# Talking-heads attention and an MLP in one kernel: relay groups of every 12th or 9th query row, and chunks of 120, 120, 120 and 97 rows

## The chip, the cores and the metric

One core of a Trainium2 chip runs the whole kernel in one launch. The metric is device time in microseconds (us) of that core: the median of three runs.

## The reference

Attention with mixed heads ("talking heads"), then a two-layer MLP with a leaky activation. 4 batches, 12 heads, 448 positions, head size 64; the MLP has 768 inputs and 2048 hidden units. All values are 32-bit floats, except the MLP weights, which the host hands over as 64-bit floats seen as pairs of integers.

```python
scores = scale * np.matmul(q, k.transpose(0, 1, 3, 2))
scores = np.einsum('bhij,hg->bgij', scores, w_pre)
scores = scores - np.max(scores, axis=-1, keepdims=True)
attn = np.exp(scores)
attn = attn / (np.sum(attn, axis=-1, keepdims=True) + 1e-09)
attn = np.einsum('bhij,hg->bgij', attn, w_post)
return np.matmul(attn, v)
...
h = x @ w_in
g = np.maximum(h, 0.0) + alpha * np.minimum(h, 0.0)
return g @ w_out
```

## The kernel before, in words

The kernel has two phases. Phase one (about the first 545 us) is the attention; phase two is the MLP on TensorE, and the change does not touch it.

In phase one the 448 query rows of a batch are cut into four **chunks** (`CHUNKS`, L27). For each chunk the scores of all 12 heads are computed in six products (`qk`, L139), two heads at a time, into PSUM with the query rows on the partitions. Each is copied to the chunk's score tile `st` (`qk_out`, L150): partition = query row of the chunk, and along the partition 12 heads of 448 scores. One partition thus holds 12 x 448 x 4 = 21,504 bytes.

The mixing of heads contracts over heads, so heads have to be on partitions. A **group** is ten query rows; its 10 x 12 = 120 rows of 448 scores are sent by one DMA, the **relay** (`relay`, L159), from ten partitions of `st` to 120 partitions of a small tile `sr`. There are 45 groups per batch, 180 in all, and eight `sr` buffers. Before the change a group's ten rows are ten neighbouring partitions, `st[r:r + 10]`. Relays alternate between the DMA queues of SP and of POOL (GpSimd); the first eight are also dealt to ACT's.

Two groups make a **block** (90 in all). For each block TensorE mixes heads (`mix`, L166, one product per half), VectorE takes the row maxima (`rmax`, L173), ScalarE the exponentials with their sums (`exp`, L178), VectorE the normalisation folded into the second mixing matrix (`norm`, L185), TensorE the second mixing, which also transposes (`post`, L196), and ScalarE copies the result into the chunk's tile `at` (`post_out`, L207), ten columns per group. When a chunk is complete, two products with v (`pv`, L216) follow, each with an output **drain** (`pv_out`, L230): ScalarE copies one PSUM half to `xe`, VectorE adds the other half, and SP stores `xe` to `x2` in DRAM.

Python code writes the order out by hand. `step(m)` issues for block m: loads due in this step, `mix(m + 1)`, stores that the step before left over, the relays up to four blocks ahead, `norm(m - 1)`, `rmax(m + 1)`, `exp(m)`, one q.k or v product with its copy, `post(m - 2)` and further products. The table `jobs`, filled from the chunks' first groups, says which step has which q.k product, v product or load. Each step also runs about 2.6 of the 224 VectorE operations that round the MLP weights (`round_f64`, L41), whose loads (`cr`, POOL's queue) and stores (`wsc`, SP's queue) go on during phase one. q.k and v products share one PSUM buffer (`ps_s`, `bufs=1`), so the next of them waits for the copy or the drain of the last.

The line of the relay, and those of the drain:

```python
dma.dma_start(out=sr_t[n][SR0:SR0 + GP], in_=s_t[ci][r:r + GI])
...
nc.scalar.copy(xe[:, :, :cn], src[:, 0, :, :cn])
nc.vector.tensor_tensor(xe[:, :, :cn], src[:, 1, :, :cn], xe[:, :, :cn], ALU.add)
```

Of the kernel before, what the change touches and what calls it, by code (L numbers as in the profile page):

```python
# [14 lines left out]
ALU = mybir.AluOpType  # L15
# [7 lines left out]
GI = 10  # L23
GP = GI * H
HI = GI // 2
HP = HI * H
CHUNKS = [(0, 110), (110, 110), (220, 110), (330, 118)]  # L27
CW = 118
NCC = DM // 128
NFC = DFF // 128  # L30
NP = H // 2
# [2 lines left out]
SR0 = 4  # L34
# [26 lines left out]
def talking_heads_prelu(ctx: ExitStack, tc: tile.TileContext, q, k, v, w_pre, w_post, mask, w_in, w_out, alpha, out):  # L61
    nc = tc.nc
# [2 lines left out]

    groups, first = [], []
    chunk_list = [(b, c) for b in range(B) for c in range(len(CHUNKS))]
    for ci, (b, c) in enumerate(chunk_list):  # L70
        first.append(len(groups))
        cn = CHUNKS[c][1]
        for r in range(0, cn, GI):
            groups.append((ci, min(r, cn - GI)))
    NG, NC = len(groups), len(chunk_list)
    NB = NG // 2
    first.append(NG)
# [34 lines left out]
    k_t, q_t, v_t, s_t, a_t = {}, {}, {}, {}, {}  # L112
# [8 lines left out]

    def load_q(ci, dmas=None):
        b, c = chunk_list[ci]
        c0, cn = CHUNKS[c]
        q_t[ci] = qp.tile([128, NP, CW], F32, tag="q", name=f"q{ci}")
        for hf in range(2):
            dma = dmas[hf] if dmas else nc.gpsimd
            dma.dma_start(out=q_t[ci][64 * hf:64 * hf + 64, :, :cn],
                          in_=q[b, :, H * c0 + NP * hf * cn:H * c0 + NP * (hf + 1) * cn])
# [7 lines left out]
    u_t = {}  # L137

    def qk(ci, p, ps_pool=None):  # L139
        b, c = chunk_list[ci]  # L140
        cn = CHUNKS[c][1]
        ps = (ps_pool or ps_s).tile([128, 2, 512], F32, tag="m" if ps_pool else "s", name=f"s{ci}_{p}")
# [7 lines left out]
    def qk_out(ci, p, copy=nc.scalar.copy):  # L150
        cn = CHUNKS[chunk_list[ci][1]][1]
        if p == 0:
            s_t[ci] = sp.tile([CW, H, S], F32, tag="s", name=f"st{ci}")
        dst = s_t[ci].rearrange("p (t n) s -> p n t s", t=2)
        copy(dst[:cn, p], u_t.pop(("qk", ci, p))[:cn, :, :S])  # L155

    sr_t, m_t, nm_t, e_t, se_t, r_t = {}, {}, {}, {}, {}, {}

    def relay(n, dma):  # L159
        ci, r = groups[n]  # L160
        sr_t[n] = sr_b[n % NSR]
        dma.dma_start(out=sr_t[n][SR0:SR0 + GP], in_=s_t[ci][r:r + GI])  # L162

    def mix(m):

# [41 lines left out]
    def post_out(m):  # L207
        for g in range(2):
            n = 2 * m + g
            ci, r = groups[n]  # L210
            if n == first[ci]:
                a_t[ci] = ap_.tile([128, NS, H, CW], F32, tag="a", name=f"at{ci}")
            dst = a_t[ci].rearrange("p s h i -> p (s h) i")[:, :, r:r + GI]
            nc.scalar.copy(dst, pa[:, g, :NS * GP].rearrange("p (s i) -> p s i", i=GI))  # L214

    def pv(ci, hx, ps_pool=None):  # L216
        b, c = chunk_list[ci]
        cn = CHUNKS[c][1]
        ps = (ps_pool or ps_s).tile([128, 2, 512], F32, tag="m" if ps_pool else "s", name=f"x{ci}_{hx}")
        for cl in range(3):  # L220
            for s in range(NS):
                for t in range(2):
                    h = 2 * (3 * hx + cl) + t
                    for r in range(2 if 2 * s + 1 < NJ else 1):
                        pr = slice(64 * r, 64 * r + 64)
                        nc.tensor.matmul(ps[64 * t:64 * t + 64, r, cl * CW:cl * CW + cn], v_t[b][pr, s, h * D:(h + 1) * D],  # L226
                                         a_t[ci][pr, s, h, :cn], start=(s == 0), stop=(2 * s + 2 + r >= NJ))
        u_t["pv", ci, hx] = ps

    def pv_out(ci, hx):  # L230
        b, c = chunk_list[ci]
        c0, cn = CHUNKS[c]
        xe = xep.tile([128, 3, CW], F32, tag="xe", name=f"xe{ci}_{hx}")
        src = u_t.pop(("pv", ci, hx))[:, :, :3 * CW].rearrange("p r (c i) -> p r c i", c=3)
        nc.scalar.copy(xe[:, :, :cn], src[:, 0, :, :cn])
        nc.vector.tensor_tensor(xe[:, :, :cn], src[:, 1, :, :cn], xe[:, :, :cn], ALU.add)  # L236
        later.append(lambda: nc.sync.dma_start(
            out=x2[3 * hx:3 * hx + 3, :, b * S + c0:b * S + c0 + cn].rearrange("c p i -> p c i"), in_=xe[:, :, :cn]))

# [32 lines left out]
    for ci, (b, c) in enumerate(chunk_list):  # L272
        if ci:
            m0, m1 = first[ci - 1] // 2 - RAHEAD, first[ci] // 2 - RAHEAD - 2
            for p in range(NP):
                at(max(m0 + p * (m1 - m0) // (NP - 1), p // 2), "qk", ci, p)
        if ci >= 2:
            at(max(first[ci - 2] // 2 - 1, 0), "load", load_q, ci)
        if c == 0:
            if b:  # L280
                at(first[ci] // 2 - 15, "load", load_k, b)
            at(first[ci] // 2 + 3 if b else 1, "load", load_v, b)
        lb = (first[ci + 1] - 1) // 2
        at(lb + LAG + 1, "pv", ci, 0)
        at(lb + LAG + (3 if ci + 1 < NC else 1), "pv", ci, 1)
    conv_steps = NFC * 2 * 7

    with tc.manual_schedule():
        p0 = ExitStack()
        start = p0.enter_context(tc.tile_pool(name="start", bufs=1))  # L290
        hw = (nc.sync, nc.scalar)
        load_q(0, hw)
        load_k(0, ((0, 1), (1, 3), (3, 6)), hw)

# [18 lines left out]
        for i, w in enumerate((w_pre, w_post)):  # L313
            for p in ((SR0, 64), (0, 64))[i]:
                nc.gpsimd.dma_start(out=mask_sb[p:p + HP, i], in_=mask[:HP, :HI, :])
                nc.gpsimd.dma_start(out=wb[p:p + HP, i, :],
                                    in_=w.rearrange("(o h) g -> o h g", o=1).to_broadcast([HI, H, H]))
        load_q(1)
        nc.gpsimd.dma_start(out=alpha_sb, in_=alpha)
        conv = convert()  # L320
        next(conv)
        nc.vector.scalar_tensor_tensor(
            out=wk[:, :HP].rearrange("p (i g) -> p i g", g=H), in0=mask_sb[:, 0], scalar=scale,
# [4 lines left out]
            out=wq.rearrange("p g i -> p i g"), in0=mask_sb[:, 1],  # L328
# [9 lines left out]
        def relays(upto, dmas):  # L338
            nonlocal relayed
            while relayed < min(upto, NG):  # L340
                relay(relayed, dmas[relayed % len(dmas)])
                relayed += 1

        relays(2 * (RAHEAD + 1), (nc.sync, nc.scalar, nc.gpsimd))
        done = 0
        live = lambda m: 0 <= m < NB
        EV = {"qk": (qk, qk_out), "pv": (pv, pv_out)}

        def step(m):
# [23 lines left out]
            if live(m - LAG):  # L373
                post(m - LAG)
                post_out(m - LAG)
# [52 lines left out]
        def l1(u):  # L428
            b, f = divmod(u, NFC)
            w, x = wi_t.pop(u), xs_t[b]  # L430
            ps = P2["h"].tile([128, 512], F32, tag="h", name=f"h{u}")
            i = 0
            for cc in range(NCC):
                for tw, tx in ((0, 0), (0, 1), (1, 0)):
                    nc.tensor.matmul(ps[:, :S], w[:, tw, cc * 128:(cc + 1) * 128], x[:, tx, cc, :],  # L435
                                     start=(i == 0), stop=(i == 3 * NCC - 1))
                    i += 1
            return ps
# [39 lines left out]
        for u in range(NU + 1):  # L478
# [5 lines left out]
            if u < NU:  # L484
                split_w(u, 1)
                ps = l1(u)
# [44 lines left out]
```

## Time and profile before

| what | value |
|---|---|
| median of 3 runs | 1043.7 us (1034.62 to 1052.75) |
| the profiled execution: its own time | 1041.12 us |
| its span, first to last instruction | 1038.9 us |
| TensorE busy over the span | 869.1 us (84%) |
| granted TensorE clock, mean | 0.921 |
| DMA packets | 55209, 123.86 MB |

The profile is of one execution. Busy times are sums of an engine's instructions; PE is TensorE's matmuls, PEld its weight loads, DVE VectorE, ACT ScalarE, POOL GpSimd. A name such as `sr<-st` says what an instruction writes and reads. "idle before" is time in which the engine did nothing just before a group's instructions, and behind it stands what ended that wait; "issue" stands where the profile shows nothing that it waited for. A DMA share is the mean busy share of the core's 16 DMA engines.

### The profile page before, as it was taken

Reading aid. Unit: us, or ns where it says so; the run is one execution under the profiler, and the core shown is the slowest. Engines: PE = TensorE matmul, PEld = TensorE weight load, DVE = VectorE, ACT = ScalarE, POOL = GpSimd, SP = SyncE. Lnnn points to the kernel's source line nnn. Section 1 sums busy time; section 2 is a strip of 40 time slices with the busy share of each in tenths; the row PEclk is TensorE's granted clock in tenths of the full one; section 3 lists DMA queues with packets and bytes.
Section 4 is the critical chain, followed back from the end, with each engine's and each line's share of the span. In section 5 each row is a group of like instructions: output and inputs, shape, how many; then the busy total and the mean of one; then the engine's idle time right before and its main releaser. Section 6 shows DMA issues by size and latency. Waiting matters only on the chain.

```text
span 1038.9 us, 26286 instructions
## 1 busy us (share of the span) xinstructions
PE 869.1 (84%) x11540; PEld 687.8 (66%) x11540; DVE 500.2 (48%) x886; ACT 441.6 (43%) x870; POOL 348.7 (34%) x305
## 2 busy tenths in 40 slices
PE   4656767867868687778666999999999999999998
PEld 2134444544535355455455999999999999999997
DVE  3454666656657376758624224632265224542222
ACT  1453666655657466648342232323233323232322
POOL 3121222222212122211004455554455454545452
PEclk9687898988889798889796999999999999999999
DMA  7698878897899977898618600020001000010001
GB/s 149 154 185 193 173 190 204 220 220 179 167 228 213 200 191 181 186 247 176 145 32 316 271 1 19 1 89 1 1 19 63 27 1 9 9 54 1 1 1 53
DMA packets 55209, 123.86 MB, mean 119 GB/s; under 512 B 21080, under 2 KB 38840, under 8 KB 54712
## 3 DMA queue, kind: packets, MB, share of 16 engines
q0 software_dynamic: 15232, 59.01, 25.7%
q1 hardware_dynamic: 38546, 60.12, 20.7%
q10 hardware_dynamic: 1318, 3.08, 1.2%
q8 instruction: 90, 1.47, 0.6%
q14 instruction: 23, 0.19, 0.1%
HBM read 59.85 MB, written 23.59 MB: 80 GB/s over the span
## 4 chain that ended last, share of the span: by engine, by line
PE 67%; DMA 16%; ACT 7%; issue 5%; DVE 4%; SPq 1%; POOL 0%; ACTq 0%; DVEq 0%; POOLq 0%
PE h L435 23%; PE acc L460 23%; DMA sr<-st 14%; PE s L147 7%; PE x L226 6%; PE m L170 4%; PE pa L204 4%; ACT st L155 3%; ACT at L214 2%; ACT e L182 1%; DMA xr<-x 1%; DMA wb<-in_w_post_dram 1%; DMA cr<-in_w_out_dram 1%; DVE xe L236 1%; DVE nm L175 1%
## 5 line engine op out<-in xcount | busy, mean ns | idle before, releaser
L435 PE MATMUL h<-xs,wi 128*128 128x448 f32 x1152 | 251.4, 371 | 12.6 <-DVE xs L425 11.3
L460 PE MATMUL acc<-g,wo 128*128 128x448 f32 x1152 | 248.2, 368 | 0.0
L435 PEld LDWEIGHTS h<-xs,wi 128*128 128x128 f32 x1152 | 218.4, 190 | 35.4 <-issue 11.5
L460 PEld LDWEIGHTS acc<-g,wo 128*128 128x128 f32 x1152 | 216.2, 188 | 21.8
L413 POOL TENSOR_TENSOR wi<-wr,wi 128x768 fp32r<-128x768 f32 x64 | 118.6, 1853 | 269.8 <-ACT wi L412 269.8
L204 PEld LDWEIGHTS pa<-r,e 64*64 64x64 f32 x5040 | 115.4, 146 | 79.6 <-issue 55.4
L175 DVE TENSOR_REDUCE nm<-m 128x2 f32<-128x896 f32 x90 | 97.9, 1088 | 135.7 <-PE m L170 135.5
L444 DVE TENSOR_SCALAR t<-h,alpha_sb 128x448 f32<-128x448 f32 x64 | 43.8, 684 | 245.7 <-PE h L435 245.7
L204 PE MATMUL pa<-r,e 64*64 64x60 f32 x5040 | 121.9, 234 | 43.6 <-issue 33.8
L170 PE MATMUL m<-sr,wk 64*64 64x448 f32 (+1 forms) x720 | 111.6, 650 | 50.4 <-DMA sr<-st 43.2
L446 ACT CAST g<-t 128x448 fp32r<-128x448 f32 x64 | 36.3, 567 | 275.2 <-DVE t L445 275.2
L162 POOL DMA_DIRECT2D sr<-st x88 | 54.2, 617 | 276.9 <-PE m L170 185.0
L147 PE MATMUL s<-k,q 64*46 64x448 f32 (+2 forms) x768 | 112.7, 640 | 39.5 <-ACT st L155 27.8
L214 ACT COPY at<-pa 128x480 f32<-128x480 f32 x180 | 93.2, 572 | 82.2 <-PE pa L204 82.0
L413 POOL TENSOR_TENSOR wo<-wr,wo 128x768 fp32r<-128x768 f32 x64 | 123.8, 1935 | 7.6 <-ACT wo L412 5.9
L182 ACT ACTIVATE e<-m,nm 128x448 f32<-128x448 f32 x180 | 113.7, 646 | 14.2 <-DVE nm L175 14.2
L226 PEld LDWEIGHTS x<-at,v 64*64 64x64 f32 x2688 | 88.2, 146 | 37.6 <-issue 20.3
L155 ACT COPY st<-s 110x896 f32<-110x896 f32 (+1 forms) x93 | 84.6, 909 | 63.0 <-PE s L147 55.6
L226 PE MATMUL x<-at,v 64*64 64x110 f32 (+1 forms) x2688 | 92.6, 280 | 18.5 <-issue 13.3
L147 PEld LDWEIGHTS s<-k,q 64*64 64x64 f32 (+2 forms) x768 | 27.5, 140 | 92.3 <-ACT st L155 70.9
L170 PEld LDWEIGHTS m<-sr,wk 64*64 64x64 f32 (+1 forms) x720 | 29.3, 151 | 77.5 <-issue 64.7
L412 ACT CAST wo<-wr 128x768 fp32r<-128x768 f32 x64 | 53.8, 841 | 62.3 <-PE acc L460 62.3
(46 smaller groups left out, 564.1 us busy)
## 6 DMA issues: line engine op xcount, KB each, us to landing
sr<-st SPq DMA_DIRECT2D x89, 210.0 KB
sr<-st POOLq DMA_DIRECT2D x88, 210.0 KB, 9.7
cr<-in_w_in_dram POOLq DMA_DIRECT2D x16, 768.0 KB, 11.5
cr<-in_w_out_dram POOLq DMA_DIRECT2D x16, 768.0 KB, 10.1
wsc<-ct SPq DMA_DIRECT2D x32, 384.0 KB
wr<-wsc SPq DMA_DIRECT2D x14, 768.0 KB
xr<-x SPq DMA_DIRECT2D x24, 224.0 KB
out_dram<-o SPq DMA_DIRECT2D x24, 224.0 KB
```

What stands on the lines that cost most here:

```text
L147: nc.tensor.matmul(ps[lo:hi, hf, :S], q_t[ci][r, p, lo:hi], k_t[b][r, p, :], start=True, stop=True)
L155: copy(dst[:cn, p], u_t.pop(("qk", ci, p))[:cn, :, :S])
L162: dma.dma_start(out=sr_t[n][SR0:SR0 + GP], in_=s_t[ci][r:r + GI])
L170: nc.tensor.matmul(ps[hf:hf + 64, u, :S], wk[r, :], g[r, :], start=True, stop=True)
L175: nc.vector.tensor_reduce(out=nm, in_=m_t[m][:, :, :S], axis=AX.X, op=ALU.max, negate=True)
L182: nc.scalar.activation(out=e_t[m][:, u], in_=m_t[m][:, u, :S], func=AF.Exp, bias=nm_t[m][:, u:u + 1], scale=1.0, accum_out=se_t[m][:, u:u ...
L204: nc.tensor.matmul(dst[:, :, HI * u:HI * u + HI], e[h, u, 64 * jb:64 * jb + 64], r[h, u].rearrange("p (h i) -> p h i", h=H), start=True, s ...
L214: nc.scalar.copy(dst, pa[:, g, :NS * GP].rearrange("p (s i) -> p s i", i=GI))
L226: nc.tensor.matmul(ps[64 * t:64 * t + 64, r, cl * CW:cl * CW + cn], v_t[b][pr, s, h * D:(h + 1) * D], a_t[ci][pr, s, h, :cn], start=(s == ...
L413: nc.gpsimd.tensor_tensor(t[:, 1], w, t[:, 0], ALU.subtract)
L435: nc.tensor.matmul(ps[:, :S], w[:, tw, cc * 128:(cc + 1) * 128], x[:, tx, cc, :], start=(i == 0), stop=(i == 3 * NCC - 1))
L460: nc.tensor.matmul(accs[c][:, :S], w[:, tw, c * 128:(c + 1) * 128], g[:, tg], start=(f == 0 and i == 0), stop=(f == NFC - 1 and i == 2))
```

## The change

The chunks become 120, 120, 120 and 97 rows. Group r of one of the first three takes the rows r, r + 12, ... r + 108: ten partitions of `st` that lie 12 apart; twelve groups fill a chunk. The fourth chunk begins at row 351; its nine groups take rows 7 + r, 16 + r, ... 88 + r of the chunk, 9 apart, and its first seven rows are computed in q.k and used by no group. There are still 45 groups per batch, 180 relays and 90 blocks. The columns of `at` now stand group by group, so the drain puts them back in order: it reads PSUM along its columns and writes `xe` in steps of 12 (or 9) elements. Two query rows (358 and 359) are computed and stored by the third and by the fourth chunk.

```diff
--- before.py
+++ after.py
@@ -24,8 +24,9 @@
 GP = GI * H
 HI = GI // 2
 HP = HI * H
-CHUNKS = [(0, 110), (110, 110), (220, 110), (330, 118)]
-CW = 118
+CHUNKS = [(0, 120), (120, 120), (240, 120), (351, 97)]
+ROWS = [(0, 12), (0, 12), (0, 12), (7, 9)]
+CW = 120
 NCC = DM // 128
 NFC = DFF // 128
 NP = H // 2
@@ -65,13 +66,13 @@
     groups, first = [], []
     chunk_list = [(b, c) for b in range(B) for c in range(len(CHUNKS))]
     for ci, (b, c) in enumerate(chunk_list):
         first.append(len(groups))
-        cn = CHUNKS[c][1]
-        for r in range(0, cn, GI):
-            groups.append((ci, min(r, cn - GI)))
+        for r in range(ROWS[c][1]):
+            groups.append((ci, r))
     NG, NC = len(groups), len(chunk_list)
     NB = NG // 2
     first.append(NG)
@@ -121,7 +122,7 @@
     def load_q(ci, dmas=None):
         b, c = chunk_list[ci]
-        c0, cn = CHUNKS[c]
+        c0, cn = sum(n for _, n in CHUNKS[:c]), CHUNKS[c][1]
         q_t[ci] = qp.tile([128, NP, CW], F32, tag="q", name=f"q{ci}")
         for hf in range(2):
             dma = dmas[hf] if dmas else nc.gpsimd
@@ -159,7 +160,9 @@
     def relay(n, dma):
         ci, r = groups[n]
         sr_t[n] = sr_b[n % NSR]
-        dma.dma_start(out=sr_t[n][SR0:SR0 + GP], in_=s_t[ci][r:r + GI])
+        r0, st = ROWS[chunk_list[ci][1]]
+        r0 += r
+        dma.dma_start(out=sr_t[n][SR0:SR0 + GP], in_=s_t[ci][r0:r0 + (GI - 1) * st + 1:st])
     def mix(m):
@@ -210,12 +213,12 @@
             ci, r = groups[n]
             if n == first[ci]:
                 a_t[ci] = ap_.tile([128, NS, H, CW], F32, tag="a", name=f"at{ci}")
-            dst = a_t[ci].rearrange("p s h i -> p (s h) i")[:, :, r:r + GI]
+            dst = a_t[ci].rearrange("p s h i -> p (s h) i")[:, :, r * GI:(r + 1) * GI]
             nc.scalar.copy(dst, pa[:, g, :NS * GP].rearrange("p (s i) -> p s i", i=GI))
     def pv(ci, hx, ps_pool=None):
         b, c = chunk_list[ci]
-        cn = CHUNKS[c][1]
+        cn = ROWS[c][1] * GI
         ps = (ps_pool or ps_s).tile([128, 2, 512], F32, tag="m" if ps_pool else "s", name=f"x{ci}_{hx}")
         for cl in range(3):
             for s in range(NS):
@@ -228,12 +231,16 @@
         u_t["pv", ci, hx] = ps
     def pv_out(ci, hx):
         b, c = chunk_list[ci]
-        c0, cn = CHUNKS[c]
+        r0, st = ROWS[c]
+        c0, cn = CHUNKS[c][0] + r0, st * GI
         xe = xep.tile([128, 3, CW], F32, tag="xe", name=f"xe{ci}_{hx}")
-        src = u_t.pop(("pv", ci, hx))[:, :, :3 * CW].rearrange("p r (c i) -> p r c i", c=3)
-        nc.scalar.copy(xe[:, :, :cn], src[:, 0, :, :cn])
-        nc.vector.tensor_tensor(xe[:, :, :cn], src[:, 1, :, :cn], xe[:, :, :cn], ALU.add)
+        ps = u_t.pop(("pv", ci, hx))[:, :, :3 * CW].rearrange("p r (c i) -> p r c i", c=3)
+        src = [ps[:, r, :, :cn].rearrange("p c (g i) -> p c g i", i=GI) for r in range(2)]
+        dst = xe[:, :, :cn].rearrange("p c (i g) -> p c g i", i=GI)
+        nc.scalar.copy(dst, src[0])
+        nc.vector.tensor_tensor(dst, src[1], dst, ALU.add)
         later.append(lambda: nc.sync.dma_start(
             out=x2[3 * hx:3 * hx + 3, :, b * S + c0:b * S + c0 + cn].rearrange("c p i -> p c i"), in_=xe[:, :, :cn]))
```

Since chunks now begin at other groups, the hand-written order moves. On TensorE, in the last blocks of the first batch's third chunk (`m` is a mixing product, `s_0` to `s_2` the first q.k products of the second batch's first chunk, `pa` the second mixing, `x_1` a v product of the second chunk); before:

```order
L147 MATMUL s_0_1173<-k_627,q_860 64x448 x2
L147 MATMUL s_0_1173<-k_627,q_860 46x448 x2
L147 MATMUL s_1_1180<-k_627,q_860 64x448 x2
L147 MATMUL s_1_1180<-k_627,q_860 46x448 x2
L170 MATMUL m_1193<-sr_116,wk 64x448 x2
L170 MATMUL m_1193<-sr_117,wk 64x448 x2
L147 MATMUL s_2_1213<-k_627,q_860 64x448 x2
L147 MATMUL s_2_1213<-k_627,q_860 46x448 x2
L204 MATMUL pa<-r_1088,e_1042 64x12x5 x28
L170 MATMUL m_1255<-sr_110,wk 64x448 x2
L170 MATMUL m_1255<-sr_111,wk 64x448 x2
L226 MATMUL x_1_1273<-at_677,v_276 64x110 x42
```

and after:

```order
L148 MATMUL s_0_1251<-k_621,q_950 64x448 x2
L148 MATMUL s_0_1251<-k_621,q_950 56x448 x2
L207 MATMUL pa<-r_1144,e_1086 64x12x5 x28
L148 MATMUL s_1_1288<-k_621,q_950 64x448 x2
L148 MATMUL s_1_1288<-k_621,q_950 56x448 x2
L148 MATMUL s_2_1294<-k_621,q_950 64x448 x2
L148 MATMUL s_2_1294<-k_621,q_950 56x448 x2
L173 MATMUL m_1302<-sr_112,wk 64x448 x2
L173 MATMUL m_1302<-sr_113,wk 64x448 x2
L229 MATMUL x_1_1320<-at_772,v_277 64x120 x42
L207 MATMUL pa<-r_1243,e_1148 64x12x5 x28
```

Before, the products s_0 to s_2 lie in two steps, with two products in the first of them; after, s_0 to s_2 lie in one step between two mixing products, with the next step's v product right behind. The number of products is the same.

On POOL's queue, around the first change of chunk (`st_184` is the first chunk's score tile, `st_262` or `st_263` the second's, `cr` a weight load, `v` the first batch's v); before:

```order
L162 DMA sr_112<-st_184 120x1x448
L162 DMA sr_115<-st_184 120x1x448
L128 DMA q_240<-in_q_dram 64x6x110 x2
L162 DMA sr_111<-st_184 120x1x448
L250 DMA cr_1_270<-in_w_out_dram 128x768
L134 DMA v_276<-in_v_dram 128x3x768
L135 DMA v_276<-in_v_dram 64x768
L162 DMA sr_113<-st_262 120x1x448
L162 DMA sr_115<-st_262 120x1x448
L162 DMA sr_117<-st_262 120x1x448
```

and after:

```order
L165 DMA sr_112<-st_184 120x1x448
L165 DMA sr_115<-st_184 120x1x448
L129 DMA q_240<-in_q_dram 64x720 x2
L165 DMA sr_111<-st_184 120x1x448
L165 DMA sr_113<-st_184 120x1x448
L257 DMA cr_1_271<-in_w_out_dram 128x768
L135 DMA v_277<-in_v_dram 128x3x768
L136 DMA v_277<-in_v_dram 64x768
L165 DMA sr_115<-st_263 120x1x448
L165 DMA sr_117<-st_263 120x1x448
```

One more relay reads the first chunk's tile, and it stands ahead of the loads of `cr` and `v`; the relays of the second chunk's tile begin one later.

## Rows read from the trace of the kernel before

**Rows 1.** The page: 40 equal slices of the span, tenths busy.

```profile
PE   4656767867868687778666999999999999999998
PEclk9687898988889798889796999999999999999999
DMA  7698878897899977898618600020001000010001
```

**Rows 2.** The page: the chain that ended last, by engine, share of the span.

```profile
PE 67%; DMA 16%; ACT 7%; issue 5%; DVE 4%; SPq 1%; POOL 0%; ACTq 0%; DVEq 0%; POOLq 0%
```

**Rows 3.** Stretches: length, busy by engine, granted clock, DMA share, GB/s.

```profile
20.00:120.00 100.00, 62.36 (x1171) 34.73 (x1175) 47.65 (x93) 45.67 (x99) 17.73 (x30) 0.80 0.81 172
120.00:220.00 100.00, 75.90 (x1907) 48.10 (x1907) 64.91 (x130) 63.45 (x141) 23.81 (x38) 0.90 0.85 206
220.00:320.00 100.00, 72.31 (x1760) 48.17 (x1761) 59.13 (x118) 56.51 (x126) 19.55 (x32) 0.86 0.86 198
320.00:420.00 100.00, 73.70 (x1814) 48.37 (x1808) 62.22 (x125) 57.84 (x129) 19.84 (x32) 0.86 0.86 193
420.00:520.00 100.00, 76.81 (x1961) 52.52 (x1959) 67.75 (x133) 59.84 (x140) 16.17 (x27) 0.87 0.80 187
520.00:545.00 25.00, 16.81 (x588) 14.47 (x579) 6.52 (x18) 11.55 (x28) 0.00 (x0) 0.93 0.11 29
```

**Rows 4.** Groups on PE, 20 to 545 us: busy, mean ns; idle before, what ended it.

```profile
L204 PE MATMUL pa<-r,e 64*64 64x60 f32 x5040 | 121.9, 234 | 43.6 <-issue 33.8 <-ACT at L214 9.5
L170 PE MATMUL m<-sr,wk 64*64 64x448 f32 (+1 forms) x720 | 111.6, 650 | 50.4 <-DMA sr<-st 43.2 <-issue 6.2
L147 PE MATMUL s<-k,q 64*46 64x448 f32 (+2 forms) x720 | 107.4, 646 | 34.7 <-ACT st L155 27.8 <-DVE r L192 3.4 <-DVE xe L236 2.5
L226 PE MATMUL x<-at,v 64*64 64x110 f32 (+1 forms) x2688 | 92.6, 280 | 18.5 <-issue 13.3 <-ACT at L214 2.0 <-ACT st L155 1.8
```

**Rows 5.** The chain, 200 to 245 us: start, length, what.

```profile
210.35 26.18 DMA sr<-st
236.53 0.14 issue
236.66 1.77 PE m L170 x8
```

**Rows 6.** DMA, 17.4 to 30 us: packets; queue: packets, MB, share of 16 engines.

```profile
DMA packets 803, 1.61 MB, mean 128 GB/s; under 512 B 136, under 2 KB 674, under 8 KB 803
q0 software_dynamic: 255, 0.69, 32.0%
q10 hardware_dynamic: 271, 0.46, 20.9%
q1 hardware_dynamic: 277, 0.47, 10.7%
```

**Rows 7.** DMA, 560 to 590 us: queue: packets, MB, share of 16 engines.

```profile
q1 hardware_dynamic: 2581, 11.82, 96.3%
```

**Rows 8.** DMA, 100 to 500 us: queue: packets, MB, share of 16 engines.

```profile
q0 software_dynamic: 12095, 47.49, 52.8%
q1 hardware_dynamic: 23734, 30.72, 30.8%
```

**Rows 9.** Timeline: PE in the middle of a v product.

```profile
308.60 0.47 PE L226 MATMUL x<-at,v 64*64 64x118 f32 x3 [4.89 <-issue]
```

**Rows 10.** Stretch 526 to 536 us, columns as in rows 3; then its DMA.

```profile
526.00:536.00 10.00, 5.36 (x248) 4.83 (x246) 1.64 (x7) 5.87 (x13) 0.00 (x0) 0.93 0.08 20
q8 instruction: 2, 0.03, 1.5%
```

**Rows 11.** Tile xe: durations ns min/median/max; and groups of two DVE setup operations.

```profile
L235 ACT COPY xe<-x x32: 434/435/455, 91.4 to 543.1; 128x330 f32<-128x330 f32 x24, 128x354 f32<-128x354 f32 x8
L236 DVE TENSOR_TENSOR xe<-x,xe x32: 491/502/528, 91.8 to 543.6; 128x330 f32<-128x330 f32 x24, 128x354 f32<-128x354 f32 x8
...
L327 DVE TENSOR_TENSOR wq<-mask_sb,wb 128x60 f32<-128x60 f32 x1 | 0.3, 266 | 0.7 <-DMA wb<-in_w_post_dram 0.7
L322 DVE SCALAR_TENSOR_TENSOR wk<-mask_sb,wb 128x60 f32<-128x60 f32 x1 | 0.2, 222 | 5.7 <-DMA q<-in_q_dram 5.7
```

## The prediction

> **What bounds the kernel now.** I read the slices of the page first. TensorE is at nine tenths or more in nearly every slice from the twenty-third on, at full granted clock, so phase two is TensorE's own time; the change does not touch it. Phase one is different: PE stands at 6 to 8 tenths, no engine is full, and the DMA share is 7 to 9 tenths throughout [rows 1]. Next the chain: DMA holds 16% of the span, "issue" 5% [rows 2], and most of the DMA part is `sr<-st`, the relay. One piece shows its kind: a relay issued at 210.35 us holds the chain for 26.18 us until a mixing product can start [rows 5]. The stretches give phase one its scale: over the five from 20 to 520 us PE is busy 361 of 500 us, ACT and DVE about 300, with a DMA share of 0.80 to 0.86 at only 172 to 206 GB/s and a granted clock of 0.80 to 0.90, mean 0.86 [rows 3].
>
> That low rate at a high share is the finding. In phase two a stretch of weight loads moves 11.82 MB at a share of 96.3% over 30 us, that is 11.82 MB in 0.963 x 16 x 30 = 462 busy engine-us, or 25.6 GB/s for each busy DMA engine [rows 7]. Between 17.4 and 30 us almost only relays run: 1.61 MB at shares of 32.0, 20.9 and 10.7%, together 63.6% of 16 engines over 12.6 us, 128 engine-us, or 12.6 GB/s [rows 6]. Relays thus get half of what a DMA engine can move. From 100 to 500 us both main queues lie at 14.0 GB/s (47.49 MB in 0.528 x 16 x 400 us) and 15.6 GB/s (30.72 MB in 0.308 of the same) [rows 8]. The relays drag the rest along.
>
> The wait reaches TensorE in two forms. The mixing product waits 43.2 us in total for `sr<-st`, and the three groups L204, L170 and L226 wait 33.8 + 6.2 + 13.3 = 53.3 us for "issue" [rows 4]. The second I also put down to DMA: in the middle of one v product PE stands still for 4.89 us although its operands are there [rows 9], in a stretch with full DMA engines, and q8, the queue that carries the engines' instructions, uses the same engines. In the quiet stretch from 526 to 536 us (share 0.08) two such instruction packets came and PE did 248 matmuls; its gaps there were ends of ACT copies [rows 10]. That code loading behind relays makes these gaps is my reading of the coincidence, not a thing the profile says.
>
> **The change part by part.** The relay. Number, bytes and issuing queues stay; what changes is where the ten source rows of 21,504 bytes lie: on ten partitions side by side, or 12 (9) apart. The trace of before has no spaced relay, so I bound the gain. No gain is possible if the slow half comes from anything but the neighbourhood of the sources. The other end is that relays are served at the 25.6 GB/s of [rows 7]. The 146 relays issued from 100 to 500 us are 31.4 MB: at 12.6 GB/s 2490 engine-us, at 25.6 GB/s 1226. Of the 0.836 x 6400 = 5350 engine-us of both queues this would free 1264, a quarter. I take a value near the full end, about 20 GB/s, since the relay-only stretch leaves little else to be slow: ten readers from ten adjacent partitions are the one thing in it that [rows 7] has not.
>
> [...]
>
> What it is worth to TensorE: of the 43.2 us of relay waits I take three quarters, **-32 us**; the rest is there because relays still queue behind loads of `cr`, k, q and v. Bounds 0 and -43. Of the 53.3 us of issue waits, 60%, **-32 us**, since the DMA share falls by about a quarter at the same pace and the shorter phase takes some of that back. Bounds 0 and -53. With shorter gaps the granted clock rises: from 0.858 to 0.90 would shorten 361 us of PE time by 17; a part lies beside ACT and DVE, so **-10 us**. Bounds 0 and -28 (the 0.93 of 520 to 545 us in [rows 3]). What comes late next is the chain of PE and ACT itself: PE waits 27.8 us for `st` copies [rows 4], and this stays.
>
> The drain. 32 pairs of one ACT copy (435 ns) and one DVE addition (502 ns) now write, and DVE also reads, in steps of 48 or 36 bytes [rows 11]. Before has no such row. The nearest: the setup operation L327, which writes in steps of 20 bytes, took 266 ns, and L322, of the same size but with packed writes, 222 [rows 11]. If all 44 ns are the step, that is 0.73 ns an element, 0.26 us for 360 elements, 0.52 us a pair, 17 us in all; the other end is nothing. Half of it lies beside other work, as the next product in the shared PSUM buffer waits for a drain only 2.5 us in all [rows 4]: **+8 us**. The upper bound for the sum is a doubling, 32 x 0.94 = 30 us, all on the path.
>
> [...] No row of before shows steps this wide.
>
> The order. Q.k products bunch up ahead of the short chunk, three in one step. Their number is the same, and each copy still ends before the next product may start; I take **+2 us**, bounds 0 and 8. The relay of the twelfth group now leads the loads of `cr` and `v` on POOL's queue instead of following later; that is no cost. The chunk of 97 rows, seven of them unused, loads 2% more q; products with 33 or 56 instead of 46 or 54 rows stream the same 448 columns, and v products sum to 450 instead of 448 columns per batch: nothing.
>
> Sum: -32 - 32 - 10 + 8 + 2 = -64. The profiled execution took 1041.1 us (its span, and 2.2 us around it), which gives 977; the median of the runs lies 2.6 us higher, so I forecast **980 us**. With all gains whole and no cost it is 1043.7 - 124 = 919.
>
> **The rivals.** (1) The relay gets no faster. It is still one DMA with ten source rows, and the 63.6% of [rows 6] is 10.2 of 16 engines: if the bound is that ten engines carry a relay, in lockstep with one another, spacing the rows helps nothing. [...] Against the rival: ten engines would still move 25.6 GB/s each, and they moved half. Time: 1043.7 + 10 = 1054.
> (2) The relay gets faster, but the in-order chain of TensorE and ScalarE takes most of it: the issue waits stay whole, and only the 43.2 us go, by three quarters, with 10 us of cost and 5 for the clock: 1043.7 - 32 - 5 + 10 = 1017. For it speaks that ACT and DVE are 60% busy and that gaps at copies remain.
> (3) Slower: the strided drain. While ACT and DVE put columns back, the one PSUM buffer is held, and the next q.k product, its copy and then the relays of the next chunk come late. It decides the sign where a pair costs 74 / 32 = 2.3 us more than its 0.94, three and a half times; at five times it costs 120 us: 1043.7 - 74 + 2 + 120 = 1092. Against it speaks the 0.73 ns above.
>
> **How the numbers follow.** My forecast holds with 0.72, its own range 930 to 1010; rival 1 with 0.10, rival 2 with 0.12, rival 3 with 0.06. A measurement of this kernel can tell about 2%, that is 21 us, from no change (the runs before span 18 us). Rival 1 lies within 2%; rival 2 straddles the line at 1023, two thirds on the faster side. So faster 0.72 + 0.08 = 0.80, same 0.10 + 0.04 = 0.14, slower 0.06. The range of 925 to 1025 leaves out rivals 1 and 3 and a little at either end.
>
> **What would show it.** Right: from 17.4 to 30 us more GB/s per DMA share; from 100 to 500 us both queues above 18 GB/s a busy engine; relay waits of L170 at 11 us or so, issue waits near 21; a clock nearer 0.90; the drain's rows under 0.8 us. Wrong: the same 12 to 14 GB/s in the relay-only stretch (rival 1); a low DMA share with issue waits as long as before (rival 2, and my reading of code loading falls); drain rows of 2 us or more with q.k waiting for `xe` (rival 3).

## The result and the profile after

The changed kernel takes 981.33 us in the median (969.51 to 982.62), against 1042.11 us for the kernel before with the runs of this comparison; the ratio is 0.9414, with a 95% interval of 0.9309 to 0.9519. In a second job on one chip it was 0.9332 (0.9260 to 0.9405). Medians hold all executions of a kernel; ratios leave out those more than 1.5% above its fastest. The forecast was 980 us. The profiled execution took 980.16 us, its span is 978.0 us, 60.9 us less than before.

The slices of the page, and the chain by engine; they answer to [rows 1, 2]:

```profile
PE   6757787677868778778649999999999999999998
...
PEclk9779899978998998999979999999999999999999
DMA  6697669676798657776069000200002000010001
...
PE 66%; ACT 10%; DMA 9%; issue 7%; DVE 7%; POOL 1%; SPq 0%; ACTq 0%; DVEq 0%; POOLq 0%
```

In phase one the DMA digits have gone from mostly 7 to 9 down to mostly 6 and 7, the clock's digits have risen, and DMA holds 9% of the chain instead of 16%. Phase one ends, with the last v product on TensorE, at 491.8 us instead of 543.0. That is 51.2 of the 60.9 us.

Most of the rest lies in phase two, which the change does not touch: from its first matmul to its last it took 480.8 us before and 471.2 us here. A stretch of it, columns as in [rows 3], before and then after:

```profile
600.00:700.00 100.00, 100.00 (x486) 90.83 (x485) 41.58 (x54) 29.94 (x43) 52.53 (x28) 1.00 0.09 28
600.00:700.00 100.00, 100.00 (x495) 92.66 (x495) 36.56 (x53) 30.41 (x44) 50.56 (x28) 1.00 0.07 24
```

TensorE is busy throughout at the same granted clock, 1.00, and yet runs 495 matmuls instead of 486. Every trace of the experiments shows one of these two lengths, near 480 or near 471 us, with either kind of relay (table below). What decides between them is not shown; these 9.6 us are not put down to the change. Whether executions without a trace differ in the same way cannot be seen. The stretches of phase one, columns as in [rows 3]:

```profile
20.00:120.00 100.00, 70.05 (x1423) 40.47 (x1426) 57.11 (x110) 55.54 (x120) 21.73 (x35) 0.81 0.78 211
120.00:220.00 100.00, 73.98 (x1970) 47.92 (x1962) 68.14 (x133) 66.14 (x143) 21.89 (x35) 0.93 0.76 208
220.00:320.00 100.00, 77.12 (x2018) 50.12 (x2016) 70.95 (x140) 67.22 (x148) 24.13 (x40) 0.91 0.79 231
320.00:420.00 100.00, 78.83 (x2009) 49.19 (x2000) 70.00 (x136) 68.19 (x147) 21.26 (x34) 0.95 0.71 206
420.00:460.00 40.00, 33.91 (x986) 24.80 (x989) 31.63 (x62) 28.69 (x68) 7.73 (x13) 0.96 0.69 220
```

More bytes move (206 to 231 GB/s against 172 to 206) at a lower share (0.69 to 0.79 against 0.80 to 0.86). That is the reading of the prediction turned round: the DMA engines do the same work in less busy time. The stretch in which almost only relays run, and the two main queues from 100 to 450 us, answer to [rows 6, 8]. DMA from 17.4 to 30 us:

```profile
DMA packets 1228, 2.47 MB, mean 196 GB/s; under 512 B 213, under 2 KB 1054, under 8 KB 1228
q0 software_dynamic: 322, 0.96, 29.2%
q1 hardware_dynamic: 524, 0.87, 25.6%
q10 hardware_dynamic: 382, 0.63, 17.6%
```

DMA from 100 to 450 us:

```profile
q0 software_dynamic: 11296, 45.10, 46.5%
q1 hardware_dynamic: 22134, 28.75, 26.2%
```

The relay stretch moves 2.47 MB in 0.724 x 16 x 12.6 = 146 busy engine-us, 16.9 GB/s for each busy engine, against 12.6 before. In the longer stretch it is 17.3 GB/s on q0 (45.10 MB in 0.465 x 5600) and 19.6 on q1, against 14.0 and 15.6. Not all of the relay stretch is relays: by size of packet they are 1.35 of the 1.61 MB before and 2.10 of the 2.47 MB after, the rest mostly loads of q. The relays' packets alone went from 12.0 to 16.9 GB/s.

What TensorE waited for, the four groups of [rows 4], from 20 us to the end of phase one:

```profile
L207 PE MATMUL pa<-r,e 64*64 64x60 f32 x5040 | 115.1, 228 | 26.2 <-issue 17.5 <-ACT at L217 8.0 <-DVE r L195 0.7
L148 PE MATMUL s<-k,q 64*64 64x448 f32 (+2 forms) x720 | 103.3, 616 | 41.1 <-ACT st L156 27.5 <-DVE xe L243 11.1 <-issue 1.9
L173 PE MATMUL m<-sr,wk 64*64 64x448 f32 (+1 forms) x720 | 102.2, 602 | 28.1 <-DMA sr<-st 18.0 <-issue 3.3 <-DVE s L191 2.8
L229 PE MATMUL x<-at,v 64*64 64x120 f32 (+1 forms) x2688 | 88.6, 273 | 22.6 <-issue 15.8 <-ACT at L217 3.4 <-ACT st L156 2.0
```

The relay wait fell from 43.2 to 18.0 us, the issue waits of the three groups from 53.3 to 36.6. The busy times of the four groups add up to 409.2 us instead of 433.5 for the same number of matmuls; counted once where matmuls overlap, PE's busy time from 20 us to the end of phase one fell from 377.9 to 356.7 us, at a mean granted clock of 0.91 instead of 0.86. The time in which PE stood still fell from 145.2 to 115.1 us. That is 30 us less, though the relay and issue waits together fell by 42: others grew, most of all that of q.k products for `xe`, the drain, from 2.5 to 11.1 us. The drain itself, answering to [rows 11]:

```profile
L242 ACT COPY xe<-x x32: 636/796/811, 76.1 to 491.8; 128x360 f32<-128x360 f32 x24, 128x270 f32<-128x270 f32 x8
L243 DVE TENSOR_TENSOR xe<-x,xe x32: 628/783/800, 76.9 to 492.5; 128x360 f32<-128x360 f32 x24, 128x270 f32<-128x270 f32 x8
...
  PE s L148: 11.1, 15
```

A pair takes 1.58 us instead of 0.94.

### The profile page after: what moved, and what is told of

Its sections match the earlier page's. It is cut to its first block, busy times and chain, and to the rows that moved or that the text cites. A ratio compares the mean times of both kernels' runs of the same rounds, so it can differ in the third digit from the quotient of the medians.

```text
span 978.0 us, 26295 instructions
## 1 busy us (share of the span) xinstructions
PE 840.5 (86%) x11540; PEld 672.4 (69%) x11540; DVE 506.6 (52%) x886; ACT 450.2 (46%) x870; POOL 347.5 (36%) x305
## 3 DMA queue, kind: packets, MB, share of 16 engines
q8 instruction: 90, 1.47, 0.7%
## 4 chain that ended last, share of the span: by engine, by line
PE 66%; ACT 10%; DMA 9%; issue 7%; DVE 7%; POOL 1%; SPq 0%; ACTq 0%; DVEq 0%; POOLq 0%
PE acc L467 24%; PE h L442 24%; DMA sr<-st 7%; PE x L229 7%; PE s L148 6%; ACT st L156 4%; ACT e L185 3%; PE m L173 3%; PE pa L207 3%; ACT at L217 2%; DVE xe L243 1%; DVE nm L178 1%; ACT xe L242 1%; DMA xr<-x 1%; DMA wb<-in_w_post_dram 1%
## 5 line engine op out<-in xcount | busy, mean ns | idle before, releaser
L442 PE MATMUL h<-xs,wi 128*128 128x448 f32 x1152 | 246.3, 367 | 12.6 <-DVE xs L432 11.1
L467 PE MATMUL acc<-g,wo 128*128 128x448 f32 x1152 | 243.7, 365 | 0.0
L207 PEld LDWEIGHTS pa<-r,e 64*64 64x64 f32 x5040 | 107.8, 139 | 58.8 <-issue 33.8
L148 PE MATMUL s<-k,q 64*64 64x448 f32 (+2 forms) x768 | 110.7, 612 | 42.6 <-ACT st L156 27.5
L207 PE MATMUL pa<-r,e 64*64 64x60 f32 x5040 | 115.1, 228 | 26.2 <-issue 17.5
L173 PE MATMUL m<-sr,wk 64*64 64x448 f32 (+1 forms) x720 | 102.2, 602 | 28.1 <-DMA sr<-st 18.0
L156 ACT COPY st<-s 120x896 f32<-120x896 f32 (+1 forms) x93 | 84.8, 912 | 67.3 <-PE s L148 55.1
L229 PEld LDWEIGHTS x<-at,v 64*64 64x64 f32 x2688 | 83.6, 141 | 41.8 <-issue 20.6
L229 PE MATMUL x<-at,v 64*64 64x120 f32 (+1 forms) x2688 | 88.6, 273 | 22.6 <-issue 15.8
L419 ACT CAST wo<-wr 128x768 fp32r<-128x768 f32 x64 | 53.5, 836 | 57.8 <-PE acc L467 57.8
L173 PEld LDWEIGHTS m<-sr,wk 64*64 64x64 f32 (+1 forms) x720 | 27.0, 144 | 55.0 <-issue 40.5
```

Source lines behind the costliest of these rows:

```text
L148: nc.tensor.matmul(ps[lo:hi, hf, :S], q_t[ci][r, p, lo:hi], k_t[b][r, p, :], start=True, stop=True)
L173: nc.tensor.matmul(ps[hf:hf + 64, u, :S], wk[r, :], g[r, :], start=True, stop=True)
L207: nc.tensor.matmul(dst[:, :, HI * u:HI * u + HI], e[h, u, 64 * jb:64 * jb + 64], r[h, u].rearrange("p (h i) -> p h i", h=H), start=True, s ...
L467: nc.tensor.matmul(accs[c][:, :S], w[:, tw, c * 128:(c + 1) * 128], g[:, tg], start=(f == 0 and i == 0), stop=(f == NFC - 1 and i == 2))
```

## The experiments

The theory: relays were slow because the ten source partitions of one relay lie side by side and, as I assumed, share a path out of the memory, which no trace names; spacing them frees DMA engines, and with them relays and, as I read it, TensorE's instruction loads. Against it stand three others: that the regrouping into twelve groups a chunk brings the gain; that only direct neighbours, or only the distance between rows, matter; that the issue waits have nothing to do with DMA. Ten runs, each with a ratio to the kernel before on the same chip. The last two columns are read from each run's one trace: where phase one ends, and how long phase two is on TensorE (before: 543.0 and 480.8; changed: 491.8 and 471.2):

| run | source rows of a relay | chunks | drain | median us | ratio to before, 95% interval | phase one ends, us | phase two, us |
|---|---|---|---|---|---|---|---|
| e1_neighbours | neighbours | changed | strided | 1039.16 | 1.0065 (0.9971 to 1.0159) | 542.3 | 480.3 |
| e3_regroup_only | neighbours | changed | packed | 1022.87 | 0.9907 (0.9844 to 0.9970) | 536.1 | 470.9 |
| e8_step2 | 2 apart | changed | strided | 1015.56 | 0.9799 (0.9731 to 0.9867) | 535.0 | 471.0 |
| e4_step8 | 8 apart | changed | strided | 994.24 | 0.9687 (0.9602 to 0.9772) | 501.0 | 480.5 |
| e10_before_step11 | 11 apart | before | packed | 987.24 | 0.9549 (0.9465 to 0.9634) | 498.3 | 471.1 |
| e9_before_step12 | 12 apart | before | packed | 980.82 | 0.9426 (0.9316 to 0.9536) | 495.7 | 471.6 |
| e5_changed_again | 12 or 9 apart | changed | strided | 974.69 | 0.9332 (0.9260 to 0.9405) | 491.2 | 471.6 |
| e2_packed_drain | 12 or 9 apart | changed | packed | 965.54 | 0.9369 (0.9239 to 0.9498) | 483.6 | 471.2 |
| e6_packed_again | 12 or 9 apart | changed | packed | 971.73 | 0.9301 (0.9222 to 0.9380) | 475.2 | 480.3 |
| e7_two_weight_loads | 12 or 9 apart | changed | strided | 931.65 | 0.8994 (0.8921 to 0.9068) | 444.0 | 471.7 |

e1 to e4 ran in one job on one chip, e5 to e8 in a second, e9 and e10 in a third; medians of different jobs are compared through the ratios. One trace shows phase one only to within several us: the changed kernel's two traces end it 0.6 us apart, those of e2 and e6, which are one kernel, 8.4.

### e1: neighbours again, all else as changed

```diff
-        r0 += r
-        dma.dma_start(out=sr_t[n][SR0:SR0 + GP], in_=s_t[ci][r0:r0 + (GI - 1) * st + 1:st])
+        r0 += r * GI
+        dma.dma_start(out=sr_t[n][SR0:SR0 + GP], in_=s_t[ci][r0:r0 + GI])
```

> The changed kernel with one edit: a relay takes ten neighbouring partitions again; chunks, groups, blocks and the strided drain stay, so the output's rows come out in another order. Theory (the spacing of the source rows brings the gain): the time returns to 1035 to 1075 us, since the costs of the change stay and its gain goes; between 17.4 and 30 us the relays move 12 to 14 GB/s for each busy DMA engine, and PE's wait for relays is 40 us or more. Rival (the regrouping into twelve groups a chunk brings the gain): 975 to 995 us.

Measured: 1039.16 us, ratio 1.0065. All of the gain is gone with this one edit. The relay stretch from 17.4 to 30 us of this run:

```profile
DMA packets 721, 1.55 MB, mean 123 GB/s; under 512 B 135, under 2 KB 588, under 8 KB 721
q0 software_dynamic: 237, 0.74, 31.8%
q10 hardware_dynamic: 267, 0.45, 22.8%
q1 hardware_dynamic: 217, 0.37, 12.7%
```

1.55 MB at shares that add to 67.3% are 11.4 GB/s for each busy engine, a little under the 12 to 14 expected, and under the 12.6 of before. The wait for relays, 28.1 us, missed the 40 us or more that were expected. The issue waits, on the other hand, are longer than before; up to 485 us, before the end of its phase one:

```profile
L207 PE MATMUL pa<-r,e 64*64 64x60 f32 x4312 | 101.3, 231 | 33.1 <-issue 29.3 <-ACT at L217 3.7
L173 PE MATMUL m<-sr,wk 60*64 60x448 f32 (+1 forms) x648 | 96.8, 621 | 42.3 <-DMA sr<-st 28.1 <-issue 7.6 <-DVE r L195 3.2
```

Over the whole of phase one the relay wait stays at 28.1 us, and the issue waits of all groups add up to 62.2 us, against 53.5 before. So the spacing is needed for the gain. The regrouping alone is the next run's question.

### e3: the regrouping alone

The edit of e1, and the drain packed:

```diff
-        src = [ps[:, r, :, :cn].rearrange("p c (g i) -> p c g i", i=GI) for r in range(2)]
-        dst = xe[:, :, :cn].rearrange("p c (i g) -> p c g i", i=GI)
+        src = [ps[:, r, :, :cn] for r in range(2)]
+        dst = xe[:, :, :cn]
```

> The change's chunks (120, 120, 120, 97), groups and blocks, but with neighbouring rows in a relay and a packed drain: the regrouping alone, and the result is the reference's. Theory (the spacing brings the gain): 1030 to 1055 us, no difference from before. Rival (the regrouping brings it): 960 to 985 us.

Measured: 1022.87 us, ratio 0.9907 (0.9844 to 0.9970): faster than before by 1%, just clear of one, and 7 us below the range. The regrouping with a packed drain brings about a sixth of the gain; with the change's own strided drain (e1) it brings nothing. Against e1 this run also shows the drain: with neighbouring rows, packing it is worth 16 us between the medians. Of the 16 us between the two traced executions, phase one holds 6 and phase two 9.

### e4 and e8: steps of 8 and of 2

Two steps between that of neighbours and 12; first 8:

```diff
-        dma.dma_start(out=sr_t[n][SR0:SR0 + GP], in_=s_t[ci][r0:r0 + (GI - 1) * st + 1:st])
+        dma.dma_start(out=sr_t[n][SR0:SR0 + GP], in_=s_t[ci][r0:r0 + (GI - 1) * 8 + 1:8])
```

and the same with 2 in place of 8.

> The changed kernel with one edit: a relay takes ten partitions 8 apart (from partition r of the chunk, or 7 + r in the last), so some rows are taken twice and others never, and the output is not the reference's; bytes, count and order of all instructions stay. If only neighbours disturb one another, it takes as long as the changed kernel: 975 to 990 us, 1792-byte relay packets near 92 ns. If rows disturb one another that share one of a few paths into the memory, also where they are not neighbours, the time lies between: 990 to 1020 us. [...]

> The changed kernel with one edit: a relay takes every second partition, r, r + 2, ... r + 18 (7 + r in the last chunk), so some rows are taken more than once, others never, and the output is not the reference's. No two rows of a relay are neighbours. If only next neighbours disturb one another: as the changed kernel, 975 to 985 us. If rows share a path in larger blocks: as the step of 8, 990 to 1010 us, 1792-byte relay packets at 100 to 120 ns. [...]

Measured: 994.24 us, ratio 0.9687, with a step of 8; 1015.56 us, ratio 0.9799, with a step of 2, some 5 us beyond the expected end. Both lie between neighbours and a step of 12, and clear of the changed kernel's 0.9414 and 0.9332. With neither step are two rows of a relay neighbours, and neither is as good as 12, so direct neighbours are not all that counts. By the ratio a step of 2 keeps a third of the gain; in its trace phase one ends only 8 us earlier than before. DMA from 17.4 to 30 us with a step of 8:

```profile
DMA packets 1038, 2.18 MB, mean 173 GB/s; under 512 B 166, under 2 KB 872, under 8 KB 1038
q0 software_dynamic: 280, 0.92, 26.3%
q1 hardware_dynamic: 414, 0.69, 22.4%
q10 hardware_dynamic: 344, 0.57, 20.1%
```

and with a step of 2:

```profile
DMA packets 784, 1.65 MB, mean 131 GB/s; under 512 B 141, under 2 KB 650, under 8 KB 784
q0 software_dynamic: 239, 0.74, 26.7%
q10 hardware_dynamic: 298, 0.50, 21.9%
q1 hardware_dynamic: 247, 0.41, 14.7%
```

That is 15.7 and 12.9 GB/s for each busy engine. The first lies between neighbours (11.4 in e1, 12.6 before) and the 16.9 of the changed kernel; the second is hardly above before.

### e9 and e10: the kernel before with spaced rows

```diff
-        dma.dma_start(out=sr_t[n][SR0:SR0 + GP], in_=s_t[ci][r:r + GI])
+        r0 = (n - first[ci]) % 2
+        dma.dma_start(out=sr_t[n][SR0:SR0 + GP], in_=s_t[ci][r0:r0 + 109:12])
```

and, for e10, `r0 = n - first[ci]` with `s_t[ci][r0:r0 + 100:11]`.

> The kernel before with one edit: a relay takes ten partitions 12 apart, from 0 and from 1 in turn, so most rows are never taken and the output is not the reference's; chunks, groups, blocks, order and the packed drain are those of before. Theory (spacing brings nearly all of the gain, the regrouping 1%): ratio to before 0.94 to 0.955, some 978 to 993 us, 1792-byte relay packets near 92 ns. Rival (spacing and regrouping need each other): ratio above 0.965.

> The kernel before with one edit: a relay takes ten partitions 11 apart, so that each row of the three chunks of 110 is taken once and the output's rows come out in another order; all else as before. [...] Theory (rows that share a path disturb one another, neighbours or not): between the step of 12 and that of 8: packets of 94 to 105 ns, ratio 0.945 to 0.97. Rival (only the distance counts): as the step of 12 in the same job.

Measured: ratio 0.9426 with 12, 0.9549 with 11. The first is the gain of the change (0.9414 and 0.9332) within the intervals, with nothing of its regrouping, so the rival that they need each other falls. Between 12 and 11 the times' intervals overlap; the packets tell them apart better. The mean duration of the relay's packets from 100 to 500 us in each trace, on SP's queue (1,792 bytes, one row of scores) and on POOL's (5,376 bytes, three):

```
source rows           before  e1   e3   step 2  step 8  step 11  step 12 (e9)  after
SP, 1792 bytes, ns    135     140  142  125     107     105      97            92
POOL, 5376 bytes, ns  487     454  454  404     333     328      295           282
```

From neighbours over 2, 8 and 11 to 12 the packets get shorter, though the three traces with neighbours scatter by 5 to 7%, so that 8 and 11 cannot be told apart. The shortest packets are 72 and 204 to 206 ns in all of these traces, 25 to 26 GB/s, the rate of [rows 7]: packets of this size can go at that rate, and it is the others that change with the step.

These packets get shorter as the step grows, which leaves the rival that only the distance counts. The changed kernel's last chunk, with its step of 9, tests it. Packets are given to relays here in the order of each queue, and the same seven groups of each batch are taken, the last chunk's without its first and last. The mean of POOL's packets is then 266 and 264 ns in the two traces of the changed kernel, 312 with a step of 8 (e4), 311 with 11 (e10) and 280 with 12 (e9); on SP it is 95 and 102 against 104, 111 and 99. A step of 9 does as well as 12 and on both queues better than 11. That speaks against distance as all that counts. Which rows share a path, if any do, is shown by no run; that a step of 11 would lie between 12 and 8 was my estimate.

### e2 and e6: the drain packed

The host lays out each chunk's query rows so that the partitions a relay takes hold ten consecutive rows; the drain as in e3:

```diff
-        "q": _np.concatenate([qt[:, :, :, a:a + n].reshape(B, D, H * n) for a, n in CHUNKS], axis=2),
+        "q": _np.concatenate([qt[:, :, :, _rows(_np, *c, *r)].reshape(B, D, H * c[1]) for c, r in zip(CHUNKS, ROWS)], axis=2),
...
+def _rows(_np, a, n, r0, st):
+    rest = _np.arange(st * GI).reshape(st, GI).T.reshape(-1)
+    return a + _np.concatenate([_np.arange(r0), r0 + rest])
```

> The changed kernel, but the host lays out each chunk's query rows so that the partitions that a relay takes (12 or 9 apart) hold ten consecutive rows; the drain then writes packed, as before the change, and the result is the reference's. Theory (half of the drain's 0.64 us a pair, 20 us in 32 pairs, was on the path): ACT copy 0.45, DVE addition 0.53 us, 971 us, between 962 and 980, 8 to 10 below the changed kernel. Rival (the drain lies beside other work): 981 us, no difference from the changed kernel. Rival (all of it is on the path): 961 us.

> The changed kernel once more, beside the others of this job on one chip. Theory: 0.94 of the time of before, some 978 to 983 us.

> The changed kernel with the query rows laid out so that the drain writes packed (as in the run e2), beside the changed kernel on the same chip. Theory (half or more of the drain's extra 20 us was on the path): 10 to 16 us below the changed kernel in the same job. Rival (it lay beside other work): within 4 us of it.

Measured: e2 965.54 us, ratio 0.9369, in a job without the changed kernel; beside it, e6 971.73 against e5 974.69 us, ratios 0.9301 (0.9222 to 0.9380) and 0.9332 (0.9260 to 0.9405). The difference of 3 us lies within the rival's 4 and below the theory's 10 to 16, but the two intervals are each about 8 us to either side, so these times decide for neither. The changed kernel itself came out somewhat faster than its expected 978 to 983 us. The drain of e6 and who waits for it:

```profile
L242 ACT COPY xe<-x x32: 384/458/461, 74.2 to 475.2; 128x360 f32<-128x360 f32 x24, 128x270 f32<-128x270 f32 x8
L243 DVE TENSOR_TENSOR xe<-x,xe x32: 429/532/534, 74.7 to 475.6; 128x360 f32<-128x360 f32 x24, 128x270 f32<-128x270 f32 x8
...
  PE s L148: 3.0, 14
```

0.59 us a pair are gone, and q.k's wait for `xe` is back from 12.2 us (e5) to 3.0, yet the time hardly moves. The traces show where it went: with the packed drain phase one ends at 483.6 (e2) and 475.2 us (e6), with the strided one at 491.8 and 491.2, so 8 and 16 us earlier; but e6's traced execution has the long phase two, 480.3 against 471.6 us in e5, and loses 9 of its 16 us there. In phase one packing is thus worth some 6 to 16 us over the three pairs, which speaks for the theory, from one trace each. That the packed layout beats the changed kernel as a whole is likely and not shown by the times.

### e7: without 30 of the 32 weight loads

```diff
-            if i < len(todo):
+            if i >= 2:
+                raw_c[i] = raw_c[i - 2]
+            else:
...
-            raw = raw_c.pop(i)
+            raw = raw_c[i]
```

> The changed kernel without 30 of the 32 loads of MLP weights in phase one: the rounding works on the first two pieces again and again, so the MLP has the wrong weights; all other instructions and DMAs stay. Theory (TensorE's issue waits are the loads of its instructions, queued behind other packets on busy DMA engines): the DMA share of 100 to 450 us falls from 0.74 to about 0.50, the issue waits on PE from 37 us to 10 to 18, the relay waits from 18 to under 12, the time by 25 to 45 us. Rival (issue waits have nothing to do with DMA): issue waits stay at 30 us or more, the time falls by less than 15 us.

Measured: 931.65 us, ratio 0.8994, below the changed kernel of the same job by 43 us in the medians and 35 by the ratios. TensorE's groups and the stretch from 100 to 420 us (share 0.59, less of a fall than expected, as the phase is shorter):

```profile
L207 PE MATMUL pa<-r,e 64*64 64x60 f32 x5040 | 110.8, 225 | 21.2 <-issue 12.1 <-ACT at L217 7.9 <-DVE r L195 1.2
L148 PE MATMUL s<-k,q 64*64 64x448 f32 (+2 forms) x720 | 98.9, 599 | 40.1 <-ACT st L156 24.7 <-DVE xe L243 14.9
L173 PE MATMUL m<-sr,wk 64*64 64x448 f32 (+1 forms) x720 | 97.5, 584 | 15.9 <-DMA sr<-st 8.2 <-issue 3.7 <-ACT e L185 2.9
L229 PE MATMUL x<-at,v 64*64 64x120 f32 (+1 forms) x2688 | 82.6, 263 | 7.8 <-ACT at L217 3.7 <-ACT st L156 2.2 <-DVE xe L243 1.4
```

```profile
100.00:420.00 320.00, 263.26 (x7251) 171.92 (x7242) 251.46 (x494) 239.56 (x522) 62.46 (x101) 0.97 0.59 177
```

Issue waits are 12.1 + 3.7 = 15.8 us, as the theory expected; the relay wait is 8.2 us and the clock 0.97. Issue waits do follow the load on the DMA engines, from 53.5 us at a share of 0.85 before to 16.0 at 0.59 here. All traces side by side, with the DMA share from 100 to 450 us (e7: to 420) and the issue waits of all PE groups in phase one:

```
                 before  e1    e3    step 11  step 2  step 8  step 12 (e9)  e6    e2    after  e5    e7
DMA share        0.85    0.82  0.84  0.81     0.80    0.78    0.78          0.77  0.76  0.74   0.74  0.59
issue waits, us  53.5    62.2  58.5  49.9     52.1    39.1    47.8          37.0  41.6  38.5   34.9  16.0
```

That it is the loading of TensorE's instructions which waits there, the prediction's reading, can be tested in the traces. The instruction queue q8 moves packets of 16,384 bytes. Of PE's pauses over 0.5 us in phase one that the profile puts to "issue", each one ends 1.15 to 1.90 us after the landing of such a packet: 20 of 20 before, 16 of 16 after, 7 of 7 here, 208 of 208 in the twelve traces. A moment picked at random in phase one lies in that span after a packet in 11 to 14% of cases, and the end of a pause of that length with another releaser in 8 to 25%. The pause of 4.89 us in [rows 9] ended at 308.60 us; its packet landed at 307.2:

```profile
q8 instruction: 1, 0.02, 4.5%
```

(DMA of the kernel before from 306 to 307.3 us, with q0 at a share of 85.0%.) These pauses hold nearly all of the issue waits, 52.5 of 53.5 us before. So the waits are for instructions. Why their packets come late beside other traffic is not shown: the packets themselves take 0.9 to 2.2 us before and 0.9 to 1.7 here.

## Why the prediction was right

The chain of effects held: spaced source rows, faster relays (12.6 to 16.9 GB/s), a less loaded DMA (0.85 to 0.74 from 100 to 450 us), shorter waits (96.5 to 54.6 us for relays and issue) and a higher clock on TensorE (0.86 to 0.91). The sum of the terms, -64 us, was meant for phase one, which ended 51.2 us earlier; that the span fell by 60.9 owes 9.6 us to phase two, which the change does not touch and the sum leaves out. Term by term the sizes were less even:

- **The relay.** "About 20 GB/s" for each busy engine: 16.9 in the relay-only stretch, 17.3 and 19.6 on the two queues. Its wait was to shrink by 32 us and shrank by 25 (43.2 to 18.0). The direction is shown by e1 and e9: neighbours take the gain away, a step of 12 in the old kernel gives all of it. The wait shrank by a fifth less than taken; relays still queue behind weight loads, and without these (e7) the wait is 8.2. That the rows of a relay share a path is shown by no run; what the runs show is the step's effect, packets of 135 to 142 ns on SP's queue with neighbours, 97 with 12 (e9) and 92 with 12 or 9. The argument that adjacent rows are the one thing that [rows 7] lacks was too short: its packets are also larger (11.82 MB in 2581, 4.6 KB each) and do not come from `st`. The shortest relay packets, at 25 GB/s, and e1 close that gap.
- **The issue waits.** Taken at -32, measured -17 (53.3 to 36.6). This is the step with the largest error. I had counted on a DMA share lower by a quarter; the shorter phase put the same bytes into less time, and the share went only from 0.80 to 0.86 down to 0.69 to 0.79. With the spacing alone (e9) the waits hardly moved, 53.5 to 47.8 us over all groups, and phase one was still 47 us shorter. e7 shows that the term was no illusion: lower the share further and the waits go to 15.8. The reading behind it, that PE waits there for its instructions, is borne out by the packets of q8.
- **The clock.** Taken at -10; PE's busy time in phase one fell by 21 us, at a granted clock of 0.81 to 0.96 per stretch, mean 0.91, close to the 0.90 assumed. I had put two fifths of the 17 us beside other work; busy time and standing still add up to the length of the phase, so all 21 count.
- **The drain.** Taken at +8 with 0.52 us a pair; 0.64 us a pair, and q.k waits for `xe` 8.6 us longer. Packing the drain ends phase one 6 to 16 us earlier in the traces; e6 against e5 shows only 3 us in the time, within the noise. The size was about right.
- **The order.** Taken at +2; e3 shows the regrouping with a packed drain to be 1% faster than before, and e9 reaches the whole gain without it. No run prices the order by itself; nothing shows that it cost more than the few us taken.

The errors of the relay and issue terms (22 us too much) and of the clock (11 too little) cancelled in part, which leaves phase one 13 us short of the sum, and phase two made up 9.6 of these. The forecast's closeness to a microsecond is luck, its sign and rough size are not.

Rival 1, that a relay remains one DMA of ten rows on ten engines and gets no faster, fell with the first profile. Rival 2, that issue waits stay whole and take most of the gain, was half right on the waits, since two thirds of them stayed, and wrong on the time. Rival 3, the slow drain, needed a pair of 3.2 us and found 1.58.

## What to carry to other kernels

In this kernel a high DMA share (0.80 to 0.86) at little more than half the GB/s for each busy engine that another stretch reached (14.0 and 15.6 on the two main queues against 25.6) was the sign that the same bytes could take less of the engines' time. Where a profile shows it, it is worth asking which partitions the sources lie on before asking for fewer bytes. For a relay between partitions it is worth trying source rows further apart; being no neighbours was not enough here (ratios of 0.9799 and 0.9687 with steps of 2 and 8, 0.9426 with 12), and which steps serve elsewhere these runs do not show. An index change does that, and the order can be put right where it is cheapest: here in the host's layout, as the strided drain cost phase one some 6 to 16 us. When transfers are freed, reckon with the faster kernel filling the engines again: here the DMA share fell only to 0.69 to 0.79, and the issue waits by 17 us where I had counted on 32.

## What the runs showed of the hardware that I had not expected

Writing 360 elements in steps of 48 bytes took ScalarE 797 ns against 458 packed (0.94 ns more per element) and VectorE, which also reads that way, 785 against 532 (0.70 ns more). These groups give the price of the stride; its cause no run here shows. First the changed kernel:

```profile
L242 ACT COPY xe<-x 128x360 f32<-128x360 f32 x24 | 19.1, 797 | 45.4 <-PE x L229 45.4
L243 DVE TENSOR_TENSOR xe<-x,xe 128x360 f32<-128x360 f32 x24 | 18.8, 785 | 47.5 <-ACT xe L242 47.4
```

and the packed medians are in the rows of e6 above.

TensorE stood still for instructions for tens of microseconds in a phase in which it runs some 18,000 matmuls and weight loads: the long pauses, 52.5 us before, each ended 1.15 to 1.90 us after a packet of q8, which moved 90 packets and 1.47 MB in the whole execution. In the stretch of [rows 10], with two such packets at a DMA share of 0.08, PE had no such pause; beside the loaded engines of this kernel it had issue waits of 53.3, 36.6 and 15.8 us at shares of 0.85, 0.74 and 0.59.
